# Sigmoid attention and a SiLU feed-forward on one core: a fixed TensorE order, a feed-forward stream between the score halves, and the first batch transposed on TensorE

## The chip, the cores and the metric

The kernel runs on one core of one Trainium2 chip. The metric is the device time of one execution in microseconds; less is better. The granted clock is the share of TensorE's full clock that its throttle lets through. PE is TensorE, ACT is ScalarE, DVE is VectorE, POOL is GpSimd, SP is the engine that issues most DMAs.

## The reference, cut to what matters

```python
# q, k, v: (8 batches, 12 heads, 448 positions, 64)
scores = q @ k.T / sqrt(64) - log(448)
attn   = 1 / (1 + exp(-scores))          # sigmoid, no softmax: no row sums
x      = (attn @ v), heads side by side  # (3584, 768)
h      = x @ w_in                        # 768 -> 2048
out    = (h * sigmoid(h)) @ w_out        # 2048 -> 768
```

Inputs and output are float32; the kernel multiplies in float16.

## The kernel before: what the change and the argument touch

The heads are taken in pairs (six per batch), so that matmuls come in twos, of 64 rows or of 64 columns each. Scores come in four chunks of 112 keys; each chunk is two matmuls and one sigmoid of 112x896 on ScalarE. Two buffers of PSUM, the memory that TensorE writes its results to, hold score chunks (`psc`), four hold everything else.

```python
def load_group(b, g):                       # two head pairs of q and of k
    ...dma_start(st, src[...])              # float32 in
    ...gpsimd.tensor_copy(x16, st)          # cast to float16
    nc.sync.dma_start_transpose(xt, x16)    # transposed by DMA

def scores(b, hp):
    for c in range(NCH):                    # 4 chunks
        psc = ps_sc.tile(...)               # bufs=2
        for j in range(2):
            nc.tensor.matmul(psc[:CP, j, :S], kT[...], qT[...])
        nc.scalar.activation(attnT[:, :, c, :], psc[...], AF.Sigmoid, ...)

def values(b, hp): ...                      # 8 matmuls, then one DVE copy to xT
def moe_h_unit(b, fc): ...                  # 6 matmuls, sigmoid on ACT, product on DVE
def moe_out_unit(m, g): ...                 # 2 x 16 matmuls, 2 DVE copies, one DMA out

for b in range(B):
    for hp in range(NPAIR):
        scores(b, hp)                       # all four chunks
        if prev is not None:
            values(*prev)                   # of the pair before
        ...                                 # loads of batch b+1, weights in batch 0
        if b > 0:
            moe_slice(b - 1, hp)            # a sixth of the feed-forward of batch b-1
```

The order in which each engine issues its instructions is not this one: a scheduler makes it at compile time.

## Time and profile before

| | |
|---|---|
| time | 482.91 us median (482.47 to 483.35, 2 runs) |
| span of the profile | 481.0 us |
| first scores | 23.06 us |
| first scores of batch 1 | 67.12 us |
| feed-forward on PE | 128 hidden units of 1.135 us and 56 halves of 2.60 us: 291 us |
| a head pair, batches 2 to 7 | 2.78 us |

The last line is worked out: from the first chunk of batch 2 (119.65 us) to the end of the last matmul (476.74 us) are 357.1 us; the feed-forward that lies in it is 112 hidden units and 50 halves, 257.1 us; the rest, divided by 36 pairs, is 2.78 us.

From the page of the kernel before: busy tenths in 40 slices of 12 us for PE and for the mean DMA engine, the granted clock, and the chain of work that ended last.

```profile
PE   0077549999999999999999999999999999999996
...
PEclk9999999999999999999999999999999999999999
DMA  9999999956744357446644375342530502011011
...
PE 78%; DMA 11%; ACT 8%; SPq 1%; issue 1%; POOL 0%; DVE 0%; POOLq 0%
```

PE is full from the seventh slice on; DMA is full in the first eight, to 96 us. PE's waits, longest first (in total us, times, longest):

```profile
PE psc_0_0_122 L115 <- DMA kT_0_85<-xk_0_82: 23.1, 1, 23.1
PE psc_0_0_323 L115 <- DMA kT_0_152<-xk_0_149: 12.2, 1, 12.2
PE psc_4_0_253 L115 <- DMA kT_2_115<-xk_2_112: 2.8, 1, 2.8
PE psc_2_0_183 L115 <- DMA kT_1_101<-xk_1_98: 2.0, 1, 2.0
```

All four are scores waiting for a transposed k. That is the start. In the steady part no wait of PE of more than 0.2 us is listed, so what a head pair costs has to be read from the timeline. One pair of batch 3, PE and the first two sigmoids (start, duration in us; a line of PE can stand for several matmuls, and an end is modelled, so read starts):

```profile
182.25 0.40 PE L115 MATMUL psc_1_0_1408<-qT_0_838,kT_0_845 64*112 64x448 f16 x2
...
182.76 0.94 PE L135 MATMUL pav_0_1425<-attnT_0_1323,v_3_831 112*64 112x448 f16 x7
182.80 1.00 ACT L122 ACTIVATE attnT_1_1407<-psc_1_0_1408,bias_s 112x896 f16<-112x896 f32 x1
...
183.69 1.01 ACT L122 ACTIVATE attnT_1_1407<-psc_1_1_1412,bias_s 112x896 f16<-112x896 f32 x1
183.85 0.40 PE L115 MATMUL psc_1_2_1416<-qT_0_838,kT_0_845 64*112 64x448 f16 x2
...
184.18 0.38 PE L135 MATMUL pav_0_1425<-attnT_0_1323,v_3_831 112*64 112x448 f16 x1
...
184.49 0.55 PE L155 MATMUL ph_4_1435<-xT_904,w_in_sb 128*128 128x448 f16 x2
...
184.97 0.40 PE L115 MATMUL psc_1_3_1420<-qT_0_838,kT_0_845 64*112 64x448 f16 x2
...
189.56 0.40 PE L115 MATMUL psc_2_0_1476<-qT_1_987,kT_1_994 64*112 64x448 f16 x2
```

The next pair starts 7.31 us later, with four hidden units (4 x 1.135 = 4.54 us) in between: the pair cost 2.77 us. Chunk 2 (psc_1_2) starts at 183.85, just after ScalarE's first sigmoid ends at 183.80 and frees its buffer; chunk 3 starts at 184.97, after the second sigmoid ends at 184.70. Meanwhile the scheduler has only an eighth values matmul and two matmuls of the next unit to put in. From 182.76 to 183.85 seven values matmuls take 1.09 us, where all eight take 0.88 us at the end of the kernel, undisturbed.

### The profile page before, as it was taken

How to read it: one execution, taken by the hardware profiler on the slowest of the kernel's cores; microseconds unless marked ns; L12 is line 12 of the kernel's file. 1: busy time of each engine (PE TensorE's matmuls, PEld its weight loads, DVE VectorE, ACT ScalarE, POOL GpSimd, SP SyncE). 2: the span in 40 equal slices, each digit the busy share in tenths (PEclk: the TensorE clock that was granted, in tenths of full speed). 3: DMA queues.
4: the chain of work that ended last, by engine and by line, in shares of the span. 5: the costliest groups of instructions: out<-in, count | busy, mean ns of one | idle time of the engine just before them, and what ended most of it. 6: DMA issues, size and time to landing. Idle time of an engine off the chain costs nothing.

```text
span 481.0 us, 6017 instructions
## 1 busy us (share of the span) xinstructions
PE 431.4 (90%) x2432; PEld 206.0 (43%) x2432; DVE 166.8 (35%) x233; ACT 244.5 (51%) x322; POOL 69.4 (14%) x116
## 2 busy tenths in 40 slices
PE   0077549999999999999999999999999999999996
PEld 0022114445444554445445544455445544455563
DVE  0012104432444225532443234523542244424521
ACT  1077426852875337762784348743772377732400
POOL 5133131111011021012101101102101000000000
PEclk9999999999999999999999999999999999999999
DMA  9999999956744357446644375342530502011011
GB/s 203 199 237 230 240 240 190 215 129 134 153 99 114 100 153 125 75 118 180 95 96 118 89 181 128 75 112 79 84 40 33 105 33 40 0 41 61 0 67 65
DMA packets 87003, 56.23 MB, mean 117 GB/s; under 512 B 46016, under 2 KB 83392, under 8 KB 86976
## 3 DMA queue, kind: packets, MB, share of 16 engines
q1 hardware_dynamic: 70848, 44.05, 37.4%
q0 software_dynamic: 16128, 11.80, 17.0%
q8 instruction: 19, 0.31, 0.3%
q14 instruction: 8, 0.07, 0.0%
HBM read 45.61 MB, written 11.01 MB: 118 GB/s over the span
## 4 chain that ended last, share of the span: by engine, by line
PE 78%; DMA 11%; ACT 8%; SPq 1%; issue 1%; POOL 0%; DVE 0%; POOLq 0%
DMA stq_2_103<-in_q_dram 3%; DMA kT_0_152<-xk_0_149 3%; DMA kT_2_115<-xk_2_112 2%; DMA stq_1_89<-in_q_dram 2%; DMA stq_0_140<-in_q_dram 1%; SPq L94 1%; PE po_1_0_3688 L173 1%; PE po_0_0_3623 L173 1%; PE po_5_0_3250 L173 1%; PE po_3_0_3147 L173 1%; PE po_1_0_2731 L173 1%; PE po_0_0_2666 L173 1%; PE po_1_0_1730 L173 1%; PE po_0_0_1665 L173 1%; PE po_5_0_1248 L173 1%
## 5 line engine op out<-in xcount | busy, mean ns | idle before, releaser
L155 PEld LDWEIGHTS <-w_in_sb 128*128 128x128 f16 x768 | 70.6, 98 | 73.8 <-issue 15.1
L173 PEld LDWEIGHTS <-gTr_3352 128*128 128x128 f16 x224 | 21.6, 98 | 14.8 <-issue 0.8
L173 PEld LDWEIGHTS <-gTr_1366 128*128 128x128 f16 x224 | 21.3, 98 | 15.1 <-issue 1.6
L173 PEld LDWEIGHTS <-gTr_365 128*128 128x128 f16 x224 | 21.3, 98 | 15.1 <-issue 1.6
L173 PEld LDWEIGHTS <-gTr_2367 128*128 128x128 f16 x224 | 21.3, 98 | 15.1 <-issue 1.6
L115 PE MATMUL psc_0_0_122<-qT_0_78,kT_0_85 64*112 64x448 f16 x2 | 0.6, 618 | 23.1 <-DMA kT_0_85<-xk_0_82 23.1
L115 PEld LDWEIGHTS <-kT_0_85 64*112 64x112 f16 x16 | 1.5, 173 | 26.6 <-DMA kT_0_85<-xk_0_82 23.1
L122 ACT ACTIVATE attnT_0_121<-psc_0_0_122,bias_s 112x896 f16<-112x896 f32 x1 | 1.0, 1007 | 21.5 <-PE psc_0_0_122 L115 21.5
L115 PE MATMUL psc_0_0_323<-qT_0_145,kT_0_152 64*112 64x448 f16 x2 | 0.6, 618 | 12.2 <-DMA kT_0_152<-xk_0_149 12.2
L143 DVE TENSOR_SCALAR xT_171<-pav_0_172 128x448 f16<-128x448 f32 x1 | 1.2, 1160 | 28.6 <-PE pav_0_172 L135 28.6
L115 PEld LDWEIGHTS <-kT_0_152 64*112 64x112 f16 x16 | 1.2, 144 | 15.7 <-DMA kT_0_152<-xk_0_149 12.6
L122 ACT ACTIVATE attnT_0_322<-psc_0_0_323,bias_s 112x896 f16<-112x896 f32 x1 | 1.0, 1007 | 12.9 <-PE psc_0_0_323 L115 12.9
L143 DVE TENSOR_SCALAR xT_171<-pav_5_339 128x448 f16<-128x448 f32 x1 | 1.1, 1150 | 17.6 <-PE pav_5_339 L135 17.6
L135 PEld LDWEIGHTS <-v_0_87 112*64 112x64 f16 x48 | 3.2, 127 | 9.2 <-issue 9.2
L163 ACT ACTIVATE tsig_0_3780<-ph_0_3773 128x448 f16<-128x448 f32 x1 | 0.5, 543 | 11.5 <-PE ph_0_3773 L155 11.5
L122 ACT ACTIVATE attnT_0_804<-psc_0_0_805,bias_s 112x896 f16<-112x896 f32 x1 | 1.0, 1007 | 9.4 <-PE psc_0_0_805 L115 9.4
L122 ACT ACTIVATE attnT_0_1805<-psc_0_0_1806,bias_s 112x896 f16<-112x896 f32 x1 | 1.0, 1007 | 9.4 <-PE psc_0_0_1806 L115 9.4
L122 ACT ACTIVATE attnT_5_2221<-psc_5_0_2222,bias_s 112x896 f16<-112x896 f32 x1 | 1.0, 1007 | 9.4 <-PE psc_5_0_2222 L115 9.4
L122 ACT ACTIVATE attnT_0_2324<-psc_0_0_2325,bias_s 112x896 f16<-112x896 f32 x1 | 1.0, 1007 | 9.4 <-PE psc_0_0_2325 L115 9.4
L122 ACT ACTIVATE attnT_0_2806<-psc_0_0_2807,bias_s 112x896 f16<-112x896 f32 x1 | 1.0, 1007 | 9.4 <-PE psc_0_0_2807 L115 9.4
L122 ACT ACTIVATE attnT_5_3222<-psc_5_0_3223,bias_s 112x896 f16<-112x896 f32 x1 | 1.0, 1007 | 9.4 <-PE psc_5_0_3223 L115 9.4
L122 ACT ACTIVATE attnT_0_3325<-psc_0_0_3326,bias_s 112x896 f16<-112x896 f32 x1 | 1.0, 1007 | 9.4 <-PE psc_0_0_3326 L115 9.4
(1056 smaller groups left out, 1016.3 us busy)
## 6 DMA issues: line engine op xcount, KB each, us to landing
w_in_sb<-in_moe_w_in_dram POOLq DMA_DIRECT2D x4, 768.0 KB, 18.5
w_out_sb<-in_moe_w_out_dram POOLq DMA_DIRECT2D x4, 768.0 KB, 14.1
v_0_87<-in_v_dram POOLq DMA_DIRECT2D x1, 672.0 KB, 14.5
v_1_138<-in_v_dram POOLq DMA_DIRECT2D x1, 672.0 KB, 17.0
v_2_349<-in_v_dram POOLq DMA_DIRECT2D x1, 672.0 KB, 18.4
v_3_831<-in_v_dram POOLq DMA_DIRECT2D x1, 672.0 KB, 6.8
v_4_1350<-in_v_dram POOLq DMA_DIRECT2D x1, 672.0 KB, 7.6
v_5_1832<-in_v_dram POOLq DMA_DIRECT2D x1, 672.0 KB, 6.9
```

The source lines that it names most:

```text
L94: nc.sync.dma_start_transpose(xt, x16.rearrange("p g c j d -> p (g c j d)"))
L115: nc.tensor.matmul(psc[:CP, j, :S], kT[j * D : (j + 1) * D, gi * NCH + c, :], qT[j * D : (j + 1) * D, gi * NCH : (gi + 1) * NCH, :], start ...
L122: nc.scalar.activation(attnT[:, :, c, :], psc[:CP, :, :S], AF.Sigmoid, bias=bias_s[:CP], scale=QKSCALE)
L135: nc.tensor.matmul(pav[j * D : (j + 1) * D, :S], v16[:, 2 * hp + j, c, :], attnT[:, j, c, :], start=(c == 0), stop=(c == NCH - 1),)
L143: nc.vector.tensor_scalar_mul(xTs[b][:, hp, :].rearrange("e (p c) -> e c p", c=NCH), pav[:, :S].rearrange("e (c p) -> e c p", c=NCH), SX,)
L155: nc.tensor.matmul(ph[:, :S], w_in_sb[:, cc, fc * P : (fc + 1) * P], xTs[b][:, cc, :], start=(cc == 0), stop=(cc == NCC - 1),)
L163: nc.scalar.activation(tsig, ph[:, :S], AF.Sigmoid, bias=0.0, scale=ISX)
L173: nc.tensor.matmul(po[:, :NO2], gTs[m][:, fc, g * P : (g + 1) * P], w_out_sb[:, fc, nh * NO2 : (nh + 1) * NO2], start=(fc == 0), stop=(fc ...
```

## The change

Its intent: give PE one program order in which it never meets ScalarE, and spare the first batch the DMA transposes it waits for. Cut to its core:

```diff
+    ctx.enter_context(tc.manual_schedule(engines={PE, Pool}))   # emission order kept
...
+    def transpose_pe(b, hp):                       # batch 0 only
+        for i, nm in enumerate("qk"):
+            eng = nc.vector if nm == "q" else nc.gpsimd
+            eng.tensor_copy(x1, st[...])           # cast
+            for c in range(NCH):
+                nc.tensor.transpose(ptr[...], x1[:, c], ident)
+            nc.vector.tensor_copy(qkT[nm, b, g][...], ptr[...])
...
-    xt = p2.tile(..., tag=f"{nm}T")                # 2 buffers
+    xt = p2.tile(..., tag=f"{nm}T", bufs=5)        # and xT bufs=3
...
+    def gemm_stream():                             # hidden units, then output halves,
+        ...                                        # yields the estimated us of each step
+    def gemm(us): ...                              # emits steps until that much is spent
...
+    stage(0, 0, split=True); load_v(0); stage(0, 1); stage(0, 2)
+    nc.gpsimd.tensor_copy(gate[:, 0:1], staged[0, 1][1][:1, 0, :1])  # POOL waits for k of group 1
+    load_weights(0)
+    for hp in range(NPAIR):                        # batch 0, no feed-forward
+        transpose_pe(0, hp); scores(0, hp, 0, 2)
+        if hp > 0: values(0, hp - 1)
+        scores(0, hp, 2, 4)
+        if hp % GP == 1:
+            stage(1, g); transpose_dma(1, g); load_weights(g + 1)
+    load_v(1); values(0, NPAIR - 1)
...
+    for n, (b, hp) in enumerate(pairs):            # batches 1 to 7
+        slot = 3.0 if b == 1 else 5.95
+        if hp % GP == 0 and b + 1 < B:
+            stage(b + 1, hp // GP); transpose_dma(b + 1, hp // GP)
+            if hp == 0: load_v(b + 1)
+        if b == 2 and hp < 4: load_weights(4 + hp) # w_out
+        scores(b, hp, 0, 2)
+        if prev is not None: values(*prev)
+        gemm(slot / 2)
+        scores(b, hp, 2, 4)
+        gemm(slot / 2)
```

More of the change, by code (lines that the diff above doesn't have):

```diff
@@ L7 @@
 from concourse.bass import ds, ts
+from concourse.masks import make_identity
 from concourse._compat import with_exitstack
@@ L36 @@
     GP = 2
-    NGRP = NPAIR // GP
     NCC = DMODEL // P
@@ L49 @@
     ps_1 = ctx.enter_context(tc.tile_pool(name="ps_1", bufs=4, space=bass.MemoryType.PSUM))
+    ctx.enter_context(
+        tc.manual_schedule(engines={mybir.EngineType.PE, mybir.EngineType.Pool})
+    )
+    qkT = {}
+    v16s = {}
+    xTs = {}
+    gTs = {}
+    attn = {}
+    staged = {}
     bias_s = cpool.tile([P, 1], F32, tag="biass", name="bias_s")
@@ L54 @@
     nc.scalar.activation(warm, bias_s, AF.Sigmoid)
+    ident = cpool.tile([P, P], F16, tag="ident", name="ident")
+    make_identity(nc, ident)
     w_in_sb = cpool.tile([P, NCC, DFF], F16, tag="w_in_sb", name="w_in_sb")
@@ L71, in load_weights, with stage, transpose_dma @@
             )
-    qkT = {}
-    v16s = {}
-    xTs = {}
-    gTs = {}
-    attn = {}
-    def load_group(b: int, g: int):
+    def stage(b: int, g: int, split: bool = False):
         h0 = 2 * GP * g
         nh = 2 * GP
-        for nm, src in (("q", q), ("k", k)):
+        tiles = []
+        for nm in ("q", "k"):
             st = p2.tile([CP, nh, NCH * D], F32, tag=f"st{nm}", name=f"st{nm}_{b}_{g}", bufs=3)
-            nc.sync.dma_start(
-                st, src[b, h0 : h0 + nh].rearrange("h (p c) d -> p h (c d)", c=NCH)
-            )
+            tiles.append(st)
+        for h in range(0, nh, 2 if split else nh):
+            hn = 2 if split else nh
+            for st, src in zip(tiles, (q, k)):
+                nc.sync.dma_start(
+                    st[:, h : h + hn],
+                    src[b, h0 + h : h0 + h + hn].rearrange("h (p c) d -> p h (c d)", c=NCH),
+                )
+        staged[b, g] = tiles
+    def transpose_dma(b: int, g: int):
+        tiles = staged.pop((b, g))
+        for nm, st in zip("qk", tiles):
             x16 = p2.tile([CP, GP, NCH, 2, D], F16, tag=f"x{nm}", name=f"x{nm}_{b}_{g}")
@@ L92, in load_group, with transpose_pe @@
                 )
-            xt = p2.tile([P, GP * NCH, CP], F16, tag=f"{nm}T", name=f"{nm}T_{b}_{g}")
-            nc.sync.dma_start_transpose(
-                xt, x16.rearrange("p g c j d -> p (g c j d)")
-            )
-            qkT[nm, b, g] = xt
+            xt = p2.tile([P, GP * NCH, CP], F16, tag=f"{nm}T", name=f"{nm}T_{b}_{g}", bufs=5)
+            nc.sync.dma_start_transpose(xt, x16.rearrange("p g c j d -> p (g c j d)"))
+            qkT[nm, b, g] = xt
+    def transpose_pe(b: int, hp: int):
+        g, gi = divmod(hp, GP)
+        for i, nm in enumerate("qk"):
+            if gi == 0:
+                qkT[nm, b, g] = p2.tile(
+                    [P, GP * NCH, CP], F16, tag=f"{nm}T", name=f"{nm}T_{b}_{g}", bufs=5
+                )
+            st = staged[b, g][i]
+            x1 = p2.tile([CP, NCH, 2, D], F16, tag=f"x1{nm}", name=f"x1{nm}_{b}_{hp}")
+            eng = nc.vector if nm == "q" else nc.gpsimd
+            eng.tensor_copy(
+                x1,
+                st[:, 2 * gi : 2 * gi + 2].rearrange("p j (c d) -> p c j d", c=NCH),
+            )
+            ptr = ps_1.tile([P, 1024], F16, tag="ps1", name=f"ptr_{b}_{hp}_{nm}")
+            for c in range(NCH):
+                nc.tensor.transpose(
+                    ptr[:, c * CP : (c + 1) * CP],
+                    x1[:, c].rearrange("p j d -> p (j d)"),
+                    ident[:CP, :CP],
+                )
+            nc.vector.tensor_copy(
+                qkT[nm, b, g][:, gi * NCH : (gi + 1) * NCH, :],
+                ptr[:, :S].rearrange("e (c p) -> e c p", c=NCH),
+            )
     def load_v(b: int):
@@ L105, in load_v, with scores @@
         v16s[b] = v16
-    def scores(b: int, hp: int):
+    def scores(b: int, hp: int, c0: int, c1: int):
         g, gi = divmod(hp, GP)
@@ L110, in scores @@
         kT = qkT["k", b, g]
-        attnT = p2.tile([CP, 2, NCH, S], F16, tag="attnT", name=f"attnT_{b}_{hp}", bufs=4)
-        for c in range(NCH):
+        if c0 == 0:
+            attn[b, hp] = p2.tile(
+                [CP, 2, NCH, S], F16, tag="attnT", name=f"attnT_{b}_{hp}", bufs=4
+            )
+        attnT = attn[b, hp]
+        for c in range(c0, c1):
             psc = ps_sc.tile([P, 2, 512], F32, tag="pssc", name=f"psc_{b}_{hp}_{c}")
@@ L124, in scores @@
             )
-        attn[b, hp] = attnT
     def values(b: int, hp: int):
@@ L130, in values @@
         if hp == 0:
-            xTs[b] = p2.tile([P, NPAIR, S], F16, tag="xT", name=f"xT_{b}")
+            xTs[b] = p2.tile([P, NPAIR, S], F16, tag="xT", name=f"xT_{b}", bufs=3)
         pav = ps_1.tile([P, 512], F32, tag="ps1", name=f"pav_{b}_{hp}")
@@ L147, in values, with h_unit @@
         )
-    def moe_h_unit(b, fc):
+    def h_unit(b, fc):
         m = b // 2
@@ L166, in moe_h_unit @@
         )
-    def moe_out_unit(m, g):
-        osb = p2.tile([P, DMODEL], F32, tag="osb", name=f"osb_{m}_{g}", bufs=3)
-        for nh in range(2):
-            po = ps_1.tile([P, 512], F32, tag="ps1", name=f"po_{m}_{g}_{nh}")
-            for fc in range(NFC):
-                nc.tensor.matmul(
-                    po[:, :NO2],
-                    gTs[m][:, fc, g * P : (g + 1) * P],
-                    w_out_sb[:, fc, nh * NO2 : (nh + 1) * NO2],
-                    start=(fc == 0),
-                    stop=(fc == NFC - 1),
-                )
-            nc.vector.tensor_scalar_mul(osb[:, nh * NO2 : (nh + 1) * NO2], po[:, :NO2], ISX)
-        nc.sync.dma_start(out[ds(m * 2 * S + g * P, P), :], osb)
@@ L183, in moe_slice @@
-    def moe_slice(b: int, sl: int):
-        if sl < 4:
-            for fc in range(4 * sl, 4 * sl + 4):
-                moe_h_unit(b, fc)
-        else:
-            m = b // 2
-            grps = [0, 1, 2] if b % 2 == 0 else [3, 4, 5, 6]
-            h = len(grps) // 2
-            for g in grps[:h] if sl == 4 else grps[h:]:
-                moe_out_unit(m, g)
-    load_group(0, 0)
-    load_v(0)
-    load_group(0, 1)
-    load_group(0, 2)
-    for s in range(4):
-        load_weights(s)
-    prev = None
@@ L201 @@
-    for b in range(B):
-        for hp in range(NPAIR):
-            scores(b, hp)
-            if prev is not None:
-                values(*prev)
-            prev = (b, hp)
-            if b + 1 < B and hp % GP == 0:
-                if hp == 0:
-                    load_v(b + 1)
-                load_group(b + 1, hp // GP)
-            if b == 0 and hp >= 2:
-                load_weights(hp + 2)
-            if b > 0:
-                moe_slice(b - 1, hp)
+    T_H = NCC * 0.189
+    T_O = NFC * 0.1625 / 2
@@ new lines, in gemm_stream @@
+    def gemm_stream():
+        for m in range(B // 2):
+            for b in (2 * m, 2 * m + 1):
+                for fc in range(NFC):
+                    h_unit(b, fc)
+                    yield T_H
+            for g in range(2 * S // P):
+                osb = p2.tile([P, DMODEL], F32, tag="osb", name=f"osb_{m}_{g}", bufs=3)
+                for nh in range(2):
+                    po = ps_1.tile([P, 512], F32, tag="ps1", name=f"po_{m}_{g}_{nh}")
+                    for fc in range(NFC):
+                        nc.tensor.matmul(
+                            po[:, :NO2],
+                            gTs[m][:, fc, g * P : (g + 1) * P],
+                            w_out_sb[:, fc, nh * NO2 : (nh + 1) * NO2],
+                            start=(fc == 0),
+                            stop=(fc == NFC - 1),
+                        )
+                        if fc == NFC // 2 - 1:
+                            yield T_O
+                    nc.vector.tensor_scalar_mul(
+                        osb[:, nh * NO2 : (nh + 1) * NO2], po[:, :NO2], ISX
+                    )
+                    yield T_O
+                nc.sync.dma_start(out[ds(m * 2 * S + g * P, P), :], osb)
@@ new lines, with gemm @@
+    stream = gemm_stream()
+    clock = [0.0, 0.0]
+    def gemm(us: float):
+        clock[1] += us
+        while clock[0] < clock[1]:
+            t = next(stream, None)
+            if t is None:
+                return False
+            clock[0] += t
+        return True
+    stage(0, 0, split=True)
+    load_v(0)
+    stage(0, 1)
+    stage(0, 2)
+    gate = cpool.tile([1, 4], F32, tag="gate", name="gate")
+    nc.gpsimd.tensor_copy(gate[:, 0:1], staged[0, 1][1][:1, 0, :1])
+    load_weights(0)
@@ new lines @@
+    for hp in range(NPAIR):
+        transpose_pe(0, hp)
+        scores(0, hp, 0, 2)
+        if hp > 0:
+            values(0, hp - 1)
+        scores(0, hp, 2, 4)
+        if hp % GP == 1:
+            g = hp // GP
+            stage(1, g)
+            transpose_dma(1, g)
+            load_weights(g + 1)
+    load_v(1)
+    values(0, NPAIR - 1)
+    pairs = [(b, hp) for b in range(1, B) for hp in range(NPAIR)]
+    prev = None
+    for n, (b, hp) in enumerate(pairs):
+        fast = b == 1
+        slot = 3.0 if fast else 5.95
+        if hp % GP == 0 and b + 1 < B:
+            stage(b + 1, hp // GP)
+            transpose_dma(b + 1, hp // GP)
+            if hp == 0:
+                load_v(b + 1)
+        if b == 2 and hp < 4:
+            load_weights(4 + hp)
+        scores(b, hp, 0, 2)
+        if prev is not None:
+            values(*prev)
+        gemm(slot / 2)
+        scores(b, hp, 2, 4)
+        gemm(slot / 2)
+        prev = (b, hp)
@@ L215 @@
     values(*prev)
-    for sl in range(NPAIR):
-        moe_slice(B - 1, sl)
+    gemm(1e9)
 _INS = ['q', 'k', 'v', 'moe_w_in', 'moe_w_out']
```

## The prediction

> **What bounds the kernel now.** TensorE: the page gives it 90% busy, and the chain of waits is 78% PE, 11% DMA, 8% ACT. From the timeline (481.0 us span):
>
> - Start, to 67.1 us: the first batch of attention, without feed-forward work. First scores at 23.06 us (wait on k's transposing DMA); later waits on such DMAs are 2.0, 2.8 and 12.2 us. The windows show DMA share above 1.1. A score matmul takes 618 ns here, 400 later, a feed-forward one 568 against 352: the array is slow until 74 us, although PEclk reads 1.0.
> - Steady state, batches 1 to 7: no PE gaps over 0.2 us. Feed-forward matmuls go at 0.189 us (x768 = 145 us) and 0.1625 us (x896 = 146 us): 291 us. A batch period is 50.2 or 55.4 us; less its 33.9 or 39.0 us of feed-forward, a head pair costs 2.73 us. Uninterrupted it would cost about 2.2 us: two score chunks 0.24 + 0.28, eight values matmuls 0.88 (measured in the last pair), two more chunks 0.56, 0.1 at each of two entries. The rest is chunks three and four waiting for ScalarE (1.0 us per sigmoid, two score buffers) while the scheduler fills in ones and twos, each change of matmul kind costing 0.1 to 0.15 us.
> - End: 4 us after the last matmul.
>
> **What changes.**
> 1. Fixed order: chunks 0,1 | previous pair's values | 3 us feed-forward | chunks 2,3 | 3 us. ScalarE gets 3 us for two sigmoids, so PE meets no wait. Estimate 2.2 instead of 2.73 us x 42 pairs: -22 us, all on the path.
> 2. Start: batch 0 loses six transposing DMAs (6.7 to 17.2 us to landing). Added per pair: two casts (0.59 us on POOL today), eight transposes, two PSUM copies. But POOL's fixed order puts the gate (k of group 1 landed: 12.3 us today, estimate 10 to 11) ahead of the first k cast, so first scores come at about 13 us. ScalarE then wants 4 x 1.01 us per pair. I expect the array still slow (attention alone never warmed it; the Trainium skill, "TensorE: Matmul & The Clock Gate", Part 4, says transpose mode does not count as busy; no trace here shows that yet), plus about 1 us of PE waiting for PSUM copies: 5.7 us per pair. Batch 1 starts at about 48 us instead of 67.
> 3. Moved: batch 1 gets 3 us of feed-forward per pair. ScalarE needs 4.03 + 2.6 x 0.54 = 5.4 us per pair against PE's 5.2: 2 to 3 us lost. v of batch 1 is issued late on POOL: 0 to 8 us of wait at the second pair. w_out is loaded only in batch 2, behind v of batch 3: 0 to 5 us at the first output group.
>
> **Sum.** 48 + 291 + 42 x 2.2 (92) + 4 + about 8 of waits = 443 us span; times run 1.9 us above the span: **445 us, range 434 to 460**. Faster by over 2%: 95%; within 2%: 4%; slower: 1%.
>
> **Signs.** Attention pair about 2.2 us in batches 3 to 6, PE idle near zero there; first scores at 13 us, held by the gate; batch 1 at 45 to 52 us; score matmuls near 600 ns in batch 0; total PE busy below 431 us.
>
> **What would make it wrong.** A clock that warms in batch 0 (total near 436). Saturated DMA making POOL's ordered casts hold up batch 0's k casts, or late transposes, v or w_out in batches 1 and 2 (455 or more). Feed-forward PSUM waiting behind attention's sigmoids.

## The result, and the profile after

The time is 449.0 us median (448.73 to 449.26, 2 runs); the ratio to before is 0.930, 95% interval 0.925 to 0.934. A ratio is the mean time of one kernel's fast runs over that of the other's of the same rounds, so not quite the ratio of the medians quoted. In a later job the same kernel took 450.16 us (448.38 to 452.45, 5 runs).

The same lines of the page, slices now of 11 us:

```profile
PE   0477839999999999999999999999999999999996
...
PEclk9998959999999999999999999999999999999999
DMA  9999999999991994089214932071011010000211
...
PE 72%; DMA 5%; POOL 1%; DVE 0%; issue 0%
```

PE is again full from the seventh slice on, but DMA is now full in the first twelve, to 134 us. PE's busy share hardly moved (90% to 91%) although the time fell by 7%. The Trainium skill, "Perfetto Trace Analysis", in the note at its head, says that matmul busy time is a bad metric for how close a kernel is to its roofline (the bound set by the hardware's peak rates), because matmuls are pipelined; these two pages of the profile agree with it.

PE's waits after:

```profile
PE ptr_0_k L131 <- POOL x1k_0_109 L125: 11.2, 1, 11.2
PE pav_0_485 L180 <- DMA v_1_399<-in_v_dram: 7.4, 1, 7.4
PE ptr_0_q L131 <- DVE x1q_0_100 L125: 4.1, 1, 4.1
PE ptr_2_k L131 <- POOL x1k_2_203 L125: 2.6, 1, 2.6
PE ptr_4_k L131 <- POOL x1k_4_306 L125: 2.2, 1, 2.2
...
PE po_0_0_1065 L228 <- DMA w_out_sb<-in_moe_w_out_dram: 0.5, 1, 0.5
```

The waits for transposed k by DMA are gone. In their place stand casts on POOL, and v of batch 1. Now the steady pair, one of batch 4, with its first two sigmoids:

```profile
206.86 0.40 PE L161 MATMUL psc_2_0_1960<-qT_1_1436,kT_1_1441 64*112 64x448 f16 x2
...
207.38 0.95 PE L180 MATMUL pav_1_1968<-attnT_1_1857,v_4_1287 112*64 112x448 f16 x8
207.41 1.00 ACT L168 ACTIVATE attnT_2_1959<-psc_2_0_1960,bias_s 112x896 f16<-112x896 f32 x1
...
208.26 1.31 PE L201 MATMUL ph_10_1978<-xT_1363,w_in_sb 128*128 128x448 f16 x6
208.30 1.01 ACT L168 ACTIVATE attnT_2_1959<-psc_2_1_1964,bias_s 112x896 f16<-112x896 f32 x1
...
210.63 0.40 PE L161 MATMUL psc_2_2_1998<-qT_1_1436,kT_1_1441 64*112 64x448 f16 x2
...
214.66 0.40 PE L161 MATMUL psc_3_0_2037<-qT_1_1436,kT_1_1441 64*112 64x448 f16 x2
```

Chunk 2 starts at 210.63, 1.3 us after the second sigmoid ended at 209.31: no wait. The next pair starts 7.80 us later with five hidden units (5.67 us) in between, so this pair cost 2.13 us. Over the whole stretch from the first chunk of batch 2 (91.48 us) to the end of the last matmul (443.25 us), 351.8 us less 272.7 us of feed-forward and 1.1 us of listed waits, it is 78.0 / 36 = 2.17 us.

The start, on PE: first scores, first scores of batch 1, the values that waited for v (since the last score matmul of 55.44 us) and what follows them.

```profile
16.88 0.62 PE L161 MATMUL psc_0_0_118<-qT_0_99,kT_0_108 64*112 64x448 f16 x2 [0.48 <-DVE kT_0_108 L136]
...
50.05 0.40 PE L161 MATMUL psc_0_0_428<-qT_0_185,kT_0_190 64*112 64x448 f16 x2
...
63.25 1.71 PE L180 MATMUL pav_0_485<-attnT_0_427,v_1_399 112*64 112x448 f16 x8 [7.41 <-DMA v_1_399<-in_v_dram]
64.89 2.42 PE L201 MATMUL ph_3_495<-xT_159,w_in_sb 128*128 128x448 f16 x6
...
68.17 1.31 PE L201 MATMUL ph_4_513<-xT_159,w_in_sb 128*128 128x448 f16 x6
```

The values matmuls of 63.25 us take 1.71 us and the hidden unit after them 2.42 us, instead of 0.95 and 1.31. The windows show why (columns: stretch, its length, busy us of PE, PEld, DVE, ACT and POOL with counts, granted clock, DMA share, GB/s):

```profile
34.00:36.00 2.00, 1.99 (x10) 0.98 (x12) 0.29 (x1) 1.57 (x3) 0.00 (x0) 1.00 1.12 304
42.00:44.00 2.00, 2.00 (x12) 0.66 (x8) 0.45 (x1) 1.52 (x2) 2.00 (x4) 0.50 1.17 160
...
60.00:62.00 2.00, 0.00 (x0) 0.00 (x0) 0.00 (x0) 0.00 (x0) 0.00 (x0) 0.50 1.47 161
66.00:68.00 2.00, 2.00 (x8) 0.55 (x6) 0.22 (x2) 0.64 (x2) 0.00 (x0) 0.50 1.25 257
68.00:70.00 2.00, 2.00 (x12) 0.99 (x11) 0.55 (x1) 2.00 (x3) 1.17 (x2) 0.96 1.29 262
```

While PE stood idle the granted clock fell to 0.50, and it came back only near 68 us. From the starts in the timeline (63.25 to 68.17 us took 4.92 us, at full clock 2.64) that cost 2.3 us beyond the 7.4 us of the wait. Note the first line: its clock reads 1.00, but its score matmuls take 0.62 us like those of 42 us, where the clock reads 0.50. The record seems to hold no value before its first change, so at the start the durations tell the clock, not the column.

In the trace the recorded clock changes at 37.43 (to full), 40.84 (to half), 44.26 (full), 57.91 (half) and 68.15 us (full). All of these lie on one grid of 3.41 us, and so do the changes in every other run of this case. So batch 0 did warm the array, in the end for its last pair. From 34.01 to 37.43 us PE ran sixteen head-pair matmuls, four or eight of a kind together and no transpose among them, and the clock rose. In the kernel before, the scheduler alternates two score and two values matmuls, twelve from 47.13 to 50.33 us, and the clock did not rise, although PE reads as busy throughout. How many it takes is not worked out here: in no_split (below) sixteen in one step of the grid did not do it.

Where the 33.5 us of span came from:

| stretch | before, us | after, us | difference |
|---|---|---|---|
| to the first scores of batch 1 | 67.12 | 50.05 | -17.1 |
| batch 1, without its feed-forward | 52.5 - 33.8 = 18.8 | 41.4 - 18.2 = 23.3 | +4.5 |
| batches 2 to 7 and the rest, without feed-forward, to the last matmul | 100.0 | 79.1 | -20.9 |
| after the last matmul | 4.3 | 4.3 | 0 |

### The profile page after: what moved, and what is told of

Read it like the earlier page. It is cut to its first block, busy times and chain, and to the rows that moved or that the text cites. A ratio compares the mean times of both kernels' runs of the same rounds, so it can differ in the third digit from the quotient of the medians.

```text
span 447.5 us, 6131 instructions
## 1 busy us (share of the span) xinstructions
PE 408.7 (91%) x2480; PEld 197.4 (44%) x2480; DVE 173.9 (39%) x251; ACT 246.1 (55%) x322; POOL 66.3 (15%) x113
## 4 chain that ended last, share of the span: by engine, by line
PE 72%; DMA 5%; POOL 1%; DVE 0%; issue 0%
DMA w_out_sb<-in_moe_w_out_dram 5%; PE po_6_1_3490 L228 1%; PE po_5_1_3425 L228 1%; PE po_4_1_3360 L228 1%; PE po_3_1_3302 L228 1%; PE po_3_0_3276 L228 1%; PE po_2_1_3237 L228 1%; PE po_0_1_3093 L228 1%; PE po_0_0_3075 L228 1%; PE po_6_0_2482 L228 1%; PE po_5_0_2403 L228 1%; PE po_4_0_2337 L228 1%; PE po_3_1_2309 L228 1%; PE po_2_0_2210 L228 1%; PE po_1_1_2171 L228 1%; PE po_1_0_2145 L228 1%
## 5 line engine op out<-in xcount | busy, mean ns | idle before, releaser
L228 PEld LDWEIGHTS <-gTr_436 128*128 128x128 f16 x224 | 20.9, 98 | 17.8 <-issue 4.9
L228 PEld LDWEIGHTS <-gTr_1537 128*128 128x128 f16 x224 | 20.9, 98 | 17.2 <-issue 4.2
L228 PEld LDWEIGHTS <-gTr_2538 128*128 128x128 f16 x224 | 20.9, 98 | 17.1 <-issue 4.2
L228 PEld LDWEIGHTS <-gTr_3517 128*128 128x128 f16 x224 | 21.9, 98 | 14.5
L168 ACT ACTIVATE attnT_0_117<-psc_0_0_118,bias_s 112x896 f16<-112x896 f32 x1 | 1.0, 1008 | 15.3 <-PE psc_0_0_118 L161 15.3
L180 PE MATMUL pav_0_485<-attnT_0_427,v_1_399 112*64 112x448 f16 x8 | 1.7, 581 | 7.4 <-DMA v_1_399<-in_v_dram 7.4
L180 PEld LDWEIGHTS <-v_1_399 112*64 112x64 f16 x48 | 2.4, 117 | 10.1 <-DMA v_1_399<-in_v_dram 7.7
L143 POOL DMA_DIRECT2D v_5_1778<-in_v_dram x1 | 0.9, 939 | 36.1 <-PE pav_5_1789 L180 36.1
L143 POOL DMA_DIRECT2D v_6_2279<-in_v_dram x1 | 0.9, 935 | 35.5 <-PE pav_5_2290 L180 35.5
L143 POOL DMA_DIRECT2D v_7_2769<-in_v_dram x1 | 0.9, 935 | 35.0 <-PE pav_5_2780 L180 35.0
L180 PEld LDWEIGHTS <-v_0_86 112*64 112x64 f16 x48 | 3.0, 142 | 5.7 <-issue 5.4
L131 PEld LDWEIGHTS <-x1k_0_109 112*128 112x128 f16 x4 | 0.3, 129 | 11.4 <-POOL x1k_0_109 L125 11.4
L188 DVE TENSOR_SCALAR xT_484<-pav_0_485 128x448 f16<-128x448 f32 x1 | 1.1, 1150 | 8.5 <-PE pav_0_485 L180 8.5
L143 POOL DMA_DIRECT2D v_4_1287<-in_v_dram x1 | 1.0, 955 | 21.2 <-PE pav_5_1298 L180 21.2
L180 PEld LDWEIGHTS <-v_7_2769 112*64 112x64 f16 x48 | 2.2, 109 | 3.0 <-issue 2.1
L180 PEld LDWEIGHTS <-v_3_783 112*64 112x64 f16 x48 | 2.2, 109 | 2.9 <-issue 2.0
L180 PEld LDWEIGHTS <-v_5_1778 112*64 112x64 f16 x48 | 2.2, 109 | 2.9 <-issue 2.0
L180 PEld LDWEIGHTS <-v_2_425 112*64 112x64 f16 x48 | 2.2, 109 | 2.9 <-issue 2.0
## 6 DMA issues: line engine op xcount, KB each, us to landing
w_out_sb<-in_moe_w_out_dram POOLq DMA_DIRECT2D x4, 768.0 KB, 15.6
v_1_399<-in_v_dram POOLq DMA_DIRECT2D x1, 672.0 KB, 19.7
```

The source lines that it names most:

```text
L131: nc.tensor.transpose(ptr[:, c * CP : (c + 1) * CP], x1[:, c].rearrange("p j d -> p (j d)"), ident[:CP, :CP],)
L143: nc.gpsimd.dma_start(v16.rearrange("p h c d -> p h (c d)"), v[b].rearrange("h (p c) d -> p h (c d)", c=NCH),)
L168: nc.scalar.activation(attnT[:, :, c, :], psc[:CP, :, :S], AF.Sigmoid, bias=bias_s[:CP], scale=QKSCALE)
L180: nc.tensor.matmul(pav[j * D : (j + 1) * D, :S], v16[:, 2 * hp + j, c, :], attnT[:, j, c, :], start=(c == 0), stop=(c == NCH - 1),)
L188: nc.vector.tensor_scalar_mul(xTs[b][:, hp, :].rearrange("e (p c) -> e c p", c=NCH), pav[:, :S].rearrange("e (c p) -> e c p", c=NCH), SX,)
L228: nc.tensor.matmul(po[:, :NO2], gTs[m][:, fc, g * P : (g + 1) * P], w_out_sb[:, fc, nh * NO2 : (nh + 1) * NO2], start=(fc == 0), stop=(fc ...
```

## The experiments

Twelve kernels ran on the chip. Each job also ran the kernel before in the same rounds (481.7 to 482.7 us median). My theory: the steady gain comes from the fixed order on PE, the start's gain from sparing batch 0 the DMA transposes, and what is still lost at the start (v, gate, casts) is lost to POOL's order. The rivals stand in each expectation.

### 1. pe_free: PE's order given back to the scheduler

```diff
-        tc.manual_schedule(engines={mybir.EngineType.PE, mybir.EngineType.Pool})
+        tc.manual_schedule(engines={mybir.EngineType.Pool})
```

> Only TensorE's fixed order is given back to the scheduler; the source order, POOL's fixed order, the start and the buffers stay. Theory (the fixed order itself is what brings a steady head pair from 2.73 to 2.19 us): the pair costs about 2.7 us again, 42 x 0.5 = 20 us more or so, about 470 us. Rival (writing the feed-forward as a stream in half steps is enough, the scheduler would follow it): 449 us, pair at 2.2 us.

Measured: 447.27 us (444.97 to 448.43, 4 runs), ratio 0.928 (0.925 to 0.931). The rival won. In the steady part the trace shows the same sequence as after: four score matmuls, eight values matmuls, half the feed-forward, four score matmuls, the other half. The pair costs 2.18 us by the same count as after. The scheduler follows a source in which nothing has to wait. It even does better in one place: it puts hidden units in front of values that wait for v, and that wait shrinks from 7.4 to 0.7 us. In another it does worse: in batch 0 it again alternates score and values matmuls by twos, the clock first changes at 56.73 us, and batch 1 starts at 53.18 us, 3.1 us later than with the fixed order.

### 2. no_split: the feed-forward not put between the score halves

```diff
         scores(b, hp, 0, 2)
         if prev is not None:
             values(*prev)
-        gemm(slot / 2)
         scores(b, hp, 2, 4)
-        gemm(slot / 2)
+        gemm(slot)
```

> The order stays fixed, but the head pair runs as chunks 0,1, values, chunks 2,3 and then all the feed-forward of the slot, not half of it between. Theory (the gain needs the 3 us of feed-forward that give ScalarE time to free the two score buffers): the third chunk comes about 1.4 us after the first, just as ScalarE frees its buffer, and the fourth waits about 0.7 us: pair near 3.0 us, 42 x 0.8 = 34 us more, about 480 us. Rival (any fixed order with the eight values matmuls together does it): within 5 us of 449.

Measured: 478.59 us (476.34 to 480.22, 4 runs), ratio 0.992 (0.988 to 0.996). PE's longest wait in this kernel, in total:

```profile
PE psc L161 <- ACT attnT L168: 22.8, 45, 1.0
```

The order is as fixed as in the change, and the time is nearly that of before only because the start keeps its gain (batch 1 at 51.56 us). The fourth chunk waits 0.5 us in every steady pair, and the third comes later as well: 2.93 us for a pair with five hidden units at 201.12 us, and 2.92 us over batches 2 to 7, more than before. So it is the 3 us between the halves that matter.

### 3. split_only: that one part alone, in the kernel before

```diff
-            scores(b, hp)
+            scores(b, hp, 0, 4 if b == 0 else 2)
             if prev is not None:
                 values(*prev)
...
             if b > 0:
-                moe_slice(b - 1, hp)
+                moe_slice(b - 1, hp, (0,))      # first half of the slice
+                scores(b, hp, 2, 4)
+                moe_slice(b - 1, hp, (1,))      # second half
```

> The kernel before with one part of the change: the head pair's chunks 2,3 come after half of its slice of feed-forward, and the scheduler stays free; the start, the DMA transposes and the buffers are those of before. Theory (half the feed-forward between the two score halves is the whole of the steady gain): a pair costs 2.2 instead of 2.73 us, 42 x 0.53 = 22 us less than before, about 460 us, with batch 1 starting at 67 us as before. Rival (it needs the fixed order, the balanced slots or a third xT buffer as well): 470 to 482 us.

Measured: 457.56 us (457.09 to 458.47, 4 runs), ratio 0.949 (0.947 to 0.951). Batch 1 starts at 65.23 us, 1.9 us earlier than in the profile of before. The rest of the 25 us lies in the pairs of batches 1 to 7. One of batch 2, on PE:

```profile
121.01 0.59 PE L117 MATMUL psc<-qT,kT 64*112 64x448 f16 x4
121.52 0.95 PE L136 MATMUL pav<-attnT,v 112*64 112x448 f16 x8
122.40 2.44 PE L156 MATMUL ph<-xT,w_in_sb 128*128 128x448 f16 x12
124.78 0.59 PE L117 MATMUL psc<-qT,kT 64*112 64x448 f16 x4
125.29 2.44 PE L156 MATMUL ph<-xT,w_in_sb 128*128 128x448 f16 x12
127.67 0.59 PE L117 MATMUL psc<-qT,kT 64*112 64x448 f16 x4
```

The next pair starts 6.66 us later, with four hidden units (4.54 us) in between: 2.12 us. Over batches 2 to 7 it is 2.18 us, less 1.4 us of listed waits, against 2.17 after. Nothing else of the change is needed for it: no fixed order, no balanced slots, no further buffers.

### 4. dma_first: batch 0 transposed by DMA again

```diff
-        transpose_pe(0, hp)
+        if hp % GP == 0:
+            transpose_dma(0, hp // GP)
```

> The first batch is transposed by DMA again, all else as after. Theory (the start gained because the first batch does without transposing DMAs in a saturated queue): batch 1 starts at 60 to 67 us instead of 50, 460 to 466 us in all. Rival (the start gained from the split loads and from holding back the weights): batch 1 at 50 to 53 us, 449 to 452 us.

Measured: 461.51 us (461.05 to 463.85, 4 runs), ratio 0.958 (0.954 to 0.961). Batch 1 starts at 65.68 us. PE's waits for transposed k are back:

```profile
PE psc L161 <- DMA kT<-xk: 39.4, 3, 25.7
```

The start's gain is the transposes on PE: 15.6 us at the start of batch 1, and 11.4 us of them at the end (against 450.16 us). Together with split_only this accounts for the result: 25.2 us there, less the 1.9 us by which its profile started batch 1 earlier, and 11.4 us here make 34.7 us; 32.6 us (later job) and 33.9 us (first job) were measured for the whole.

### 5. v_early: v of batch 1 issued earlier

```diff
             transpose_dma(1, g)
+            if g == 0:
+                load_v(1)
             load_weights(g + 1)
-    load_v(1)
     values(0, NPAIR - 1)
```

> The load of v for batch 1 is issued after the first staged group of batch 1 (about 27 us) instead of at 43.5 us. Theory (the 7.4 us wait for it at 55.8 us and the slow clock after it, about 2 us, are on the path): 9 us less, about 440 us. Rival (the DMA queues are saturated, so the wait moves to the transposes or to the k casts of batch 0): 446 to 450 us.

Measured: 451.88 us (448.05 to 453.85, 4 runs), ratio 0.936 (0.931 to 0.941): nothing gained. Batch 2 started at 84.0 us instead of 91.5, but then:

```profile
PE po L228 <- DMA w_out_sb<-in_moe_w_out_dram: 7.4, 2, 3.8
```

The 7.4 us came back at the first output group, as a wait for w_out, and the slow clock came back with it (half from 115.44 to 125.68 us).

### 6. after_again: the changed kernel unedited

> The changed kernel once more, unedited, as the yardstick of these runs: about 449 us.

Measured: 450.16 us (448.38 to 452.45, 5 runs), ratio 0.934 (0.930 to 0.937).

### 7. k_dve: batch 0's k casts on VectorE

```diff
-            eng = nc.vector if nm == "q" else nc.gpsimd
+            eng = nc.vector
```

> In the changed kernel the k casts of batch 0 go to VectorE (0.43 us there) instead of POOL, so neither the gate nor POOL's casts for batch 1 hold them up. Theory (POOL's order costs batch 0 its late start at 16.9 us and the two waits of 2.6 and 2.2 us): first scores at 7 to 8 us, batch 1 at about 38 us. If that is on the path, about 438 us. Rival (DMA is saturated for the first 120 us, and what is won at the start is waited for later, at v, transposes, weights or w_out): PE's wait for DMA grows by what the start won, 445 to 450 us.

Measured: 451.2 us (450.31 to 455.76, 5 runs), ratio 0.937 (0.933 to 0.941). Batch 1 started at 39.3 us, 10.8 us earlier than after, and all of it was given back:

```profile
PE pav L180 <- DMA v<-in_v_dram: 13.6, 1, 13.6
PE psc L161 <- DVE kT L136: 10.6, 6, 7.9
...
PE po L228 <- DMA w_out_sb<-in_moe_w_out_dram: 3.9, 1, 3.9
```

PE waited 13.6 us for v (7.4 after) and 3.9 us for w_out (0.5 after), and the clock fell to half during both (from 49.65 to 63.31 and from 117.92 to 124.75 us). First scores came at 13.6 us, not at 7 to 8: VectorE's scheduled order had casts that wait for loads in front of the copy that the first scores wait for (7.9 us). So POOL's order was not what the start hung on alone.

### 8. vw_early: v and w_out both earlier

On top of v_early:

```diff
-        if b == 2 and hp < 4:
-            load_weights(4 + hp)
+        if b == 1 and hp >= 2:
+            load_weights(2 + hp)
```

> v of batch 1 early as in v_early, and the four w_out loads in batch 1 (about 65 to 80 us) instead of batch 2 behind the load of v that waits for TensorE. Theory (in v_early the 7.4 us came back as a wait for w_out because of POOL's order): no wait for w_out, b 2 at 84 us, about 441 us. Rival (there the DMA itself was full): the wait comes back at the transposes or weights of batches 1 and 2, 447 to 452 us.

Measured: 440.4 us (439.95 to 446.41, 5 runs), ratio 0.916 (0.911 to 0.922); the changed kernel in the same rounds has 0.934. PE waits for no load of v or weights. In the changed kernel POOL issued the w_out loads only at 94.7 us, behind a load of v whose buffer the values of batch 1 freed at 93.8 us; here they go at 68.4 and 84.2 us. The first output group starts at 109.7 us and waits for nothing. This beats both kernels.

### 9. all_free: no fixed order on any engine

```diff
-    ctx.enter_context(
-        tc.manual_schedule(engines={mybir.EngineType.PE, mybir.EngineType.Pool})
-    )
```

> The changed kernel without any fixed order, on TensorE or POOL; all else as after. Theory after pe_free (the fixed order brings nothing; source order, split and transposes do): 444 to 450 us. Rival (POOL's fixed order is worth something, since it keeps batch 0's casts ahead of later loads): 455 us or more.

Measured: 446.65 us (445.25 to 447.27, 4 runs), ratio 0.926 (0.924 to 0.928). The fixed order of either engine brings nothing to the total. What TensorE's brings at the start (batch 1 at 50.05 us instead of 53.29) is lost again in the wait for v, 7.4 us after and 0.8 us here.

### 10. no_gate: vw_early without the gate

```diff
-    gate = cpool.tile([1, 4], F32, tag="gate", name="gate")
-    nc.gpsimd.tensor_copy(gate[:, 0:1], staged[0, 1][1][:1, 0, :1])
```

> vw_early without the gate, so w_in's first quarter is issued at about 2.6 us and no k cast waits for k of group 1. Theory (the gate costs batch 0 some 9 us at its start, but the DMA queues are full, so little of it reaches the end): first scores at 8 to 9 us, POOL's casts for batch 1 then hold up the third pair; 436 to 440 us against 440. Rival (the gate protects the first loads: without it they land late): 442 us or more.

Measured: 445.23 us (443.22 to 450.31, 5 runs), ratio 0.923 (0.920 to 0.925): 4.8 us above vw_early by the medians, though the two intervals overlap a little. In the profiles batch 1 starts at 56.1 us instead of 50.6, and from there on both take nearly the same time (387.0 and 387.6 us). First scores came at 13.0 us, later than I expected, for the same reason as in k_dve, and then POOL's casts for batch 1, behind their loads, held the third and the fifth pair up by 6.9 and 8.2 us (3.3 and 1.8 in vw_early). The gate, which I had counted as a cost only, is worth its price here. Why is not shown: POOL got k of the second group of batch 1 at 43.1 us instead of 38.0, and whether the weights issued at 2.6 us delayed it no run here tells.

### 11. best: vw_early, k casts on VectorE, w_out two pairs earlier

```diff
-            eng = nc.vector if nm == "q" else nc.gpsimd
+            eng = nc.vector
...
-        if b == 1 and hp >= 2:
-            load_weights(2 + hp)
+        if b == 1 and hp in (1, 3):
+            load_weights(4 + hp - 1)
+            load_weights(4 + hp)
```

> vw_early with the k casts of batch 0 on VectorE and the w_out loads two pairs earlier. Theory (with v and w_out issued early the start won by k_dve, 10 us, is no longer given back at v; DMA, full until all of w_out has landed, keeps a part): batch 1 at about 39 us, 431 to 437 us. Rival (DMA alone sets when the first output group can start, about 105 us, so nothing is won): 439 to 441 us.

Measured: 443.46 us (439.36 to 447.33, 5 runs), ratio 0.916 (0.912 to 0.919): as vw_early. Batch 1 starts at 40.3 us, but PE then waits for transposed k in batch 1 (4.7 us) and in batch 2 (6.6 us):

```profile
PE psc L161 <- DMA kT<-xk: 11.3, 2, 6.6
```

What was won at the start moved once more, now to the transposing DMAs.

### 12. light: best with three quarters of the weight loads left out (wrong result)

```diff
     def load_weights(step: int):
+        if step % 4:
+            return
...
-                w_in_sb[:, cc, fc * P : (fc + 1) * P],
+                w_in_sb[:, cc, fc % 4 * P : (fc % 4 + 1) * P],
...
-                            w_out_sb[:, fc, nh * NO2 : (nh + 1) * NO2],
+                            w_out_sb[:, fc % 4, nh * NO2 : (nh + 1) * NO2],
```

> The kernel of the run best with a wrong result on purpose: only the first quarter of w_in and of w_out is loaded and used again for the other quarters, so TensorE's work is the same and six weight loads of 768 KB (some 30 us of full DMA, an estimate from DMA windows of about 230 GB/s in written bytes and twice that in read ones) are gone. Theory (the DMA engines being full in the first 120 us is what gave the start's gain back, in best as 11 us of waits for transposed k and the slow clock after them): those waits shrink to under 2 us and the time falls to 427 to 433 us. Rival (it is the order on the queues, each transposing DMA waiting for the one before, and not the volume): the waits stay, 440 us or more.

Measured: 429.05 us (427.77 to 429.71, 5 runs), ratio 0.889 (0.887 to 0.891); the result is wrong, as meant. Every wait of PE for a DMA is gone; its longest waits are these two:

```profile
PE psc L163 <- DVE kT L138: 11.4, 6, 8.6
PE ptr_q L133 <- DVE x1q L127: 4.1, 1, 4.1
```

The first of them is the copy of k on VectorE behind casts that wait for the very first loads. PE does the same work in both kernels. With less to move, the start's gain reaches the end. So in best it is the weight loads that take it away. The page shows DMA full for fifteen slices, to 166 us, in best and for ten, to 107 us, in light, so a full DMA alone does not make PE wait. The edit takes away the bytes and their places in POOL's queue together; it does not part the two. (The six loads write 4.7 MB, some 20 us at the 230 GB/s of the expectation; its 30 us was high.) For the changed kernel itself this test was not run; that its waits move in the same way is shown by v_early and k_dve.

## Why the prediction was right, and where it was not

- **Time.** 445 us with 434 to 460 was predicted, 449.0 us measured. By its terms: batch 1 at 48 us was predicted and 50.05 measured, 92 + 8 us for 42 pairs and waits and 102.3 measured, 291 and 4 as they came. The sum is not luck, except inside batch 0 (below).
- **Steady pair.** 2.2 us was predicted and 2.17 us measured, against 2.78 us before by the same count. The mechanism named first (PE meets no wait because ScalarE gets 3 us for two sigmoids) is shown by no_split and split_only.
- **The step that failed**: "Fixed order: ... PE meets no wait." The order did not have to be fixed. pe_free and all_free keep the steady gain with a free scheduler. What counts is that half the feed-forward stands between the score halves in the source.
- **First scores.** 13 us was predicted, "held by the gate"; 16.88 us was measured and the gate held them. The term that was mis-sized is the landing of k of group 1: estimated at 10 to 11 us, POOL saw it at 14.2 us (12.3 us before). The two loads of group 2 and one of batch 1 had been issued by then too; whether they delayed it no run here tells.
- **Batch 0.** 5.7 us per pair was predicted and (50.05 - 16.88) / 6 = 5.5 us measured. The sum is close but its parts are not those predicted: 4.7 us of the 33.2 are two waits for POOL's k casts, which stood among the dangers, not in the sum; the four pairs without such a wait took 4.6 to 4.9 us. So a late start and pairs shorter than expected cancelled in part, which is luck.
- **Clock.** Score matmuls near 600 ns in batch 0 were predicted and seen until 44 us. My ground for it, that attention alone never warms the array, was wrong. The recorded clock rose at 37.43 us, fell in the wait for the fifth pair's k cast and rose again at 44.26; the last pair ran at 0.40 us a line. In k_dve it rose at 22.35 us. In all the kernels with a fixed order on TensorE it rose before batch 1; in the four with a free one (before, split_only, pe_free, all_free), which alternate by twos, only after batch 1 had started, at 56.7 to 74.6 us. That the matmuls of one kind standing together are the cause was not tested alone.
- **Batch 1.** The loss to ScalarE was put at 2 to 3 us; PE's waits for sigmoids there are three of 0.35 us, and one more at the start of batch 2. The wait for v was put at 0 to 8 us and was 7.4; the 2.3 us of slow clock after it were not in the sum. The wait for w_out was put at 0 to 5 us and was 0.5; v_early shows that it was small only because PE came late.
- **Where the rest stays.** POOL's order did cost batch 0 its time (k_dve: batch 1 10.8 us earlier), but undoing it did not shorten the kernel. In vw_early one order on POOL did: the w_out loads no longer stand behind a load of v that waits for its buffer. For what best then still loses, light shows the weight loads as the cause.

## What to carry to other kernels

If a producer and a consumer share few buffers, put enough independent work between the halves of the producer in the source, and check the scheduler's order before fixing one by hand. In a start where DMA is full, an earlier start of one engine may only move its waits to a later load; sort the loads by the time at which each is first needed, and look for one that stands in a queue behind another that waits for a buffer. After a change, add up the waits anew: one that reads 0.5 us may be 7 us as soon as another is gone.

## What the Trainium skill lacked or had wrong

- "TensorE: Matmul & The Clock Gate", Part 1, says that the window in which activity is judged is about 3.4 us long and free-running, that is, it does not start anew with the work. The runs agree: the changes of the granted clock at 37.43, 40.84, 44.26, 57.91 and 68.15 us lie 3.41 us or a multiple of it apart. So the clock could fall 2.1 us after PE went idle at 55.8 us, and come back 4.9 us after work began at 63.25. The step of the grid that ended in the fall, 54.49 to 57.91 us, held 1.0 us of work, so such a step need not be wholly idle. What the page lacks is which activity counts as busy: in the kernel before PE was busy without a pause from 45 to 52 us with head-pair matmuls only, in twos, and they stayed at 0.62 us a line; in the changed kernel the same matmuls, in fours and eights, brought the full clock after 3.4 us (34.01 to 37.43 us).
- The same page, Part 4, says that transpose mode doesn't count as PE-busy in the same way. In dma_first, which has no transpose on PE, the clock rose at 64.67 us, before any feed-forward (66.19 us), so transposes are not needed for it; whether they count stays open. The page gives about 390 ns for one transpose of 128x128 alone and 275 ns in one kernel; here, from the start of four of 112x112 in a row to the start of the next matmul, they took 0.35 us in all at the slow clock (20.06 to 20.41 us) and 0.21 us at the fast one (44.34 to 44.55 us).
- "Trainium Kernel Development and Optimization", Key Constraints, says that the DMAs of all queues run on the same 16 engines and interleave. The runs agree: in light fewer loads on POOL's queue did away with 11.3 us of waits for transposes on SP's. They add the size: a load of v of the same 672 KB took 19.7 us to land in the full start and 7.1 us later, a transposing DMA up to 24.6 us in the start of the kernel before and 3.0 us later. No page that I looked up gives a way to estimate the landing of a DMA among so many others.
- No page that I looked up says that the granted clock has no record before its first change: it reads 1.00 at 34 us, where the score matmuls take 0.62 us as they do under a clock of 0.50.
